# Gated attention and a token/channel mixer on one core: another order of token and channel products, and of SyncE's queue

## Chip, core and metric

The kernel runs on one core of one Trainium2 chip. The metric is the device time of one execution in microseconds, the median of several; less is better. A core has TensorE (PE in the profile, its weight loads PEld), VectorE (DVE), ScalarE (ACT), GpSimd (POOL) and SyncE (SP), each with an instruction queue of its own that it works off in order, and DMA engines that SyncE's and GpSimd's queues feed. TensorE writes its results to PSUM, from where VectorE and ScalarE take them to SBUF.

## What is computed

For each of 8 batches, an attention without softmax, gated by u, and then an MLP mixer over tokens and channels:

```python
def _attn_ref(u, v, z):                       # u, v: 8 x 3008 x 256; z: 8 x 3008 x 64
    scores = (1.0 / S) * np.matmul(z, z.transpose(0, 2, 1))
    attn = np.maximum(scores, 0.0) ** 2
    return u * np.matmul(attn, v)

def _moe_ref(x, w_tok1, w_tok2, w_ch1, w_ch2):  # token width 256, channel width 1536
    xt = x.transpose(0, 2, 1)
    h = np.maximum(xt @ w_tok1, 0.0) @ w_tok2
    u = x + h.transpose(0, 2, 1)
    return u + np.maximum(u @ w_ch1, 0.0) @ w_ch2
```

## The kernel before

**Tiles.** The 3008 rows of a batch are six query blocks of 512 (the last 448), `q` = 0 to 5 (`NQ` = 6), and as many key groups. Everything runs in bf16 with float32 sums in PSUM. PSUM is handed out in pairs of banks: a ring of three pairs, and a fourth after the first block (`ring`, `take_slot`, `bank_pair`).

**Attention.** For a query block TensorE makes the scores of a key group (`score_run`, L464), ScalarE takes them through relu (`relu`, L490 and L502), VectorE squares them (L510, L541), and TensorE multiplies by v (`av_matmul`, L691). Since scores are symmetric, only half of the blocks are computed. The others are *mirror blocks*: SyncE issues a DMA transpose of a finished block (`flip`, L561), and of the tiles under the diagonal of a diagonal block (`flip_tiles`, L553). A finished query block is gated with u (`gate`, L845): its result is kept transposed in xT, and SyncE issues a transpose of it for the token products (`turn_x`, L882). u comes by GpSimd's queue (`load_u`, L255) and is transposed on SyncE's queue too (`turn_u`, L265).

**Mixer.** For each batch: the first token product, one *piece* for each query block, all six summing into one PSUM pair (`tok1`, L1024); VectorE collects it (`collect_a`, L1040 to L1050, into a_sb); the second token product, one piece for each query block (`tok2`, L1068), which VectorE adds to xT (L1077); that sum is transposed back on SyncE's queue (`turn_u2`, L1096). Then, for each query block, six channel pieces (`ch1`, L1124, evacuated through relu into h2pre at L1162, or L1164 on VectorE) and the second channel product. The first token product and the second channel product are done with seven block products in place of eight, from sums that VectorE makes beforehand (`x_sums`, L919; `make_sums`, L1203 to L1215). The seven channel products are `product(q, k)`, L1252, in the order 1, 2, 6, 5, 7, 3, 4. They sum into two PSUM pairs: 1, 6, 7 and 4 into xb, 2, 5 and 3 into zb. After each of them VectorE adds its result to ro (`collect`, L1289), and products 6, 5, 7, 3 and 4 wait for the add on an earlier one in the same pair. The 64 odd rows at the end of a batch go by plain products (`ch2`, L1338; *residual-row pieces* below): one piece for an even batch, two for an odd one, whose second takes the rows of two batches (hs). The last query block of the last batch goes wholly by `ch2`.

**Who decides the order.** The program has no loop on the chip. A planner in Python emits all instructions in an order that it works out with costs and due times of its own. Work for VectorE, ScalarE and SyncE is put into a waiting list with `push(engine, ready, busy, latency, fn, first=...)`. `next_op` takes the item that can start first; among equals the higher `first`, then the earlier `ready`. Mixer work for TensorE stands in two lists of pieces, worked off in turn: `heads` (tok1, tok2) and `tails` (ch1, the products, ch2). `next_piece` chooses between the heads of the two lists: the list that did not go last is asked first. A piece may *open* a group that holds PSUM (the first tok1 piece, product 1) and another *closes* it (the last tok1 piece, product 4). While a group is open, its list is asked first, and no other group may open. Between the blocks of attention the planner stops for mixing at `goal`: from batch 2 on, ahead of block (b, 0), it does the pieces of query blocks 3 to 5 of batch b-2, then tok1, tok2 and query blocks 0 to 2 of batch b-1. Batch 7 is mixed at the end, and batches 0 and 1 within batch 1 and ahead of batch 2.

**So the order around the change** is, for batches 1 to 7: the products of block 4 of the batch before, with ch1 pieces of its block 5 among them; then six tok1 pieces in a run; the last ch1 piece of block 5; its ch2 pieces; then tok2 pieces of the new batch in turn with the seven products of block 5; then ch1 pieces of block 0. In `add_mixer` the tails of a block are laid down by the tuple `(0, 0, 1, 2, 0, 6, 5, 0, 7, 3, 0, 4)`, where a number is a product and 0 stands for a ch2 piece, as long as there is one, and for a ch1 piece of the next block otherwise.

Of the very last ch1 piece (batch 7, block 5) VectorE evacuates one half (L1146) and ScalarE the other (L1144). On SyncE's queue `turn_x` has `first=1`, mirror blocks have 0. `turn_u` is not put into the waiting list but emitted as soon as it is due, from the list `later`.

Of the kernel before, what the change touches and what calls it, by code (L numbers as in the profile page):

```python
# [13 lines left out]
P = 128  # L14
# [43 lines left out]
def kernel(  # L58
# [203 lines left out]
    def turn_u(b, q):  # L262
# [5 lines left out]
        on_sp(1.25)  # L268
# [566 lines left out]
    def gate(blk, dh, acc, t):  # L835
# [97 lines left out]
    opened = [None]  # L933
    before = [None]
# [58 lines left out]

    def add_mixer(b):
# [6 lines left out]
        def tok1(q, end):  # L1001
# [28 lines left out]
            if q == NQ - 1:  # L1030
                home = "fl" if b else "h2"

                def collect_a(t):
# [5 lines left out]
                    def both(to, ps, k):  # L1039
# [10 lines left out]
                    nc.vector.tensor_single_scalar(  # L1050
                        st["a"].rearrange("p m d -> p (m d)"),
                        f[:, 0:4, :].rearrange("p k d -> p (k d)"), 0.0, AX.max)
                    recent[0] = st["a"][:, 0, :1]
                    a_done.t = t
                    if b:
                        release("fl", [1], t)
                    else:
                        live["h2"] -= 1
# [53 lines left out]
        def ch1(q, c2, borrowed, end):  # L1112
            slot, _ = take_slot()
# [6 lines left out]
            hp = bank_pair(slot, "hp")  # L1120
            for r in range(2):
                cc = 2 * c2 + r
                for dc in range(DT):
                    nc.tensor.matmul(  # L1124
                        hp[:, r, :W], w_ch1_sb[:, dc, cc * P:(cc + 1) * P],
# [13 lines left out]
            if (b, q, c2) == (B - 1, NQ - 1, CHT // 2 - 1):  # L1139
                landed, freed = [], Done()  # L1140

                def evacuate_part(r, t):
                    if r:
                        nc.scalar.activation(h2[:, r, :W], hp[:, r, :W], ACT.Relu)  # L1144
# [9 lines left out]
                ring.append((freed, slot))  # L1154
# [4 lines left out]
            def evacuate(t):  # L1159
# [7 lines left out]
                if fast(q) and c2 % 2:  # L1167
                    if borrowed and q == HALF and b < B - 1:
                        late_sums.append(lambda t: make_sums(q, c2 // 2, t))
                    else:  # L1170
# [3 lines left out]
                              done=h2_done[q, c2]), slot))  # L1174
# [44 lines left out]

        def bank_of(q, k):  # L1220
# [629 lines left out]
```

## Time and profile before

| | us |
|---|---|
| median of three runs | 1124.84 (1124.3 to 1125.99) |
| the profiled execution | 1123.19 |
| its span, first to last instruction | 1121.4 |
| VectorE busy in the span | 782.4 |
| ScalarE busy in the span | 654.1 |

The profile comes from one execution. A row of the timeline has the start, the length to the end of the last instruction in it, engine, line, operation, tiles and shapes, a count, and in brackets the idle time of the engine before it with what ended it. A matmul's row reaches past the start of the next one, because matmuls are pipelined, so the length of a stretch is read from start to start. Rows of the view by stretches have the stretch, its length, the busy time and number of instructions of PE, PEld, DVE, ACT and POOL, the granted clock of TensorE, the share of the DMA engines and their GB/s. Rows of waits have who waited for whom, the total, how often and the longest. A row that ends in `x48: a/b/c, d to e` has the least, median and greatest duration in ns and the first and last start in us. SPq rows are issues of DMAs from SyncE's queue.

### The profile page before, as it was taken

What the parts mean: (1) busy time and instruction counts of PE and PEld (TensorE: products, weight loads), DVE (VectorE), ACT (ScalarE), POOL (GpSimd) and SP (SyncE); (2) the same over time, 40 slices, a digit from 0 to 9 for tenths busy, and PEclk for the clock granted to TensorE, in tenths of its full rate; (3) what the DMA queues carried; (4) which work ended last, traced back from release to release, by engine and by line L of the source; (5) the groups of instructions that cost most, each with busy time, mean ns of one, the idle gap of its engine ahead of it and who ended that gap; (6) DMA issues with size and microseconds to landing.
All of it is one profiled execution on the core that took longest, in us unless ns stands there. A gap on an engine that the chain in (4) does not pass through costs nothing.

```text
span 1121.4 us, 26909 instructions
## 1 busy us (share of the span) xinstructions
PE 1110.3 (99%) x10965; PEld 676.5 (60%) x10965; DVE 782.4 (70%) x1849; ACT 654.1 (58%) x817; POOL 164.7 (15%) x388
## 2 busy tenths in 40 slices
PE   9999999999999999999999999999999999999997
PEld 3444574766557665576555765557655576556676
DVE  6889847775757857678557775678756776557764
ACT  7998525545844467545665356753666526743363
POOL 5321100211003110031100320013200110000000
PEclk9999999999999999999999999999999999999999
DMA  9999945696986969769597896958969869684223
GB/s 177 168 185 167 203 108 124 123 167 134 191 147 130 194 119 190 141 128 205 129 173 126 149 191 141 176 117 147 209 129 159 134 145 180 131 166 96 53 77 76
DMA packets 466156, 165.52 MB, mean 148 GB/s; under 512 B 433072, under 2 KB 449008, under 8 KB 466032
## 3 DMA queue, kind: packets, MB, share of 16 engines
q1 hardware_dynamic: 436640, 131.11, 58.8%
q0 software_dynamic: 28880, 32.32, 20.8%
q8 instruction: 85, 1.39, 0.5%
q14 instruction: 39, 0.32, 0.1%
q10 hardware_dynamic: 512, 0.38, 0.1%
HBM read 65.40 MB, written 24.64 MB: 80 GB/s over the span
## 4 chain that ended last, share of the span: by engine, by line
PE 91%; DVE 4%; DMA 2%; SPq 1%; ACT 1%; issue 1%; POOL 0%; ACTq 0%; DVEq 0%; POOLq 0%
PE acc L691 39%; PE hp L1124 22%; PE xb L1252 9%; PE zb L1252 7%; PE sc L464 6%; PE a_ps L1024 3%; PE op L1338 3%; PE h_ps L1068 2%; DVE xT L1077 2%; DMA fl<-at 1%; PE first_acc L608 1%; DMA v_sb<-in_v_dram 1%; DVE res L1373 0%; ACT at L502 0%; DVE ro L1289 0%
## 5 line engine op out<-in xcount | busy, mean ns | idle before, releaser
L1162 ACT ACTIVATE h2pre<-hp 128x1024 bf16<-128x1024 f32 (+1 forms) x277 | 267.7, 1011 | 262.7 <-PE hp L1124 223.4
L691 PEld LDWEIGHTS <-v_sb 64*128 64x128 bf16 x4418 | 240.3, 94 | 217.4 <-issue 1.1
L691 PE MATMUL acc<-at,v_sb 64*128 64x512 bf16 (+1 forms) x2738 | 339.1, 374 | 0.0
L502 ACT ACTIVATE at<-sc 128x1024 bf16<-128x1024 f32 (+1 forms) x290 | 287.2, 1027 | 74.9 <-PE sc L464 56.8
L510 DVE TENSOR_TENSOR at<-at 128x1024 bf16<-128x1024 bf16 (+1 forms) x290 | 198.3, 688 | 107.4 <-ACT at L502 101.4
L1124 PE MATMUL hp<-xT,w_ch_sb 128*128 128x512 bf16 (+1 forms) x1152 | 270.6, 375 | 0.3
L691 PE MATMUL acc<-fl,v_sb 64*128 64x512 bf16 (+1 forms) x1680 | 192.1, 367 | 0.5 <-ACT at L502 0.5
L1124 PEld LDWEIGHTS <-w_ch_sb 128*128 128x128 bf16 x1152 | 105.9, 98 | 99.7 <-issue 2.6
L464 PE MATMUL sc<-zT 64*128 64x512 bf16 (+1 forms) x732 | 131.6, 359 | 1.0 <-ACT at L502 0.7
L1252 PEld LDWEIGHTS <-hsum 128*128 128x128 bf16 x1944 | 115.9, 98 | 20.1 <-issue 0.2
L1252 PEld LDWEIGHTS <-h2pre 128*128 128x128 bf16 x1458 | 88.8, 98 | 18.9
L819 ACT COPY cp<-acc 128x512 f32<-128x512 f32 (+1 forms) x94 | 54.8, 583 | 73.8 <-PE acc L691 61.4
L825 DVE TENSOR_TENSOR cp<-acc,cp 128x512 f32<-128x512 f32 (+1 forms) x94 | 63.5, 676 | 38.8 <-ACT cp L819 38.4
L1203 DVE TENSOR_TENSOR hsum<-h2pre 128x512 bf16<-128x512 bf16 (+1 forms) x132 | 53.2, 407 | 41.3 <-ACT h2pre L1162 37.1
L490 ACT ACTIVATE at<-sc 128x512 bf16<-128x512 f32 (+3 forms) x152 | 56.0, 444 | 41.5 <-PE sc L464 38.9
L1252 PE MATMUL xb<-w_mix_sb,hsum 128*128 128x128 bf16 x972 | 68.6, 219 | 0.0
L464 PEld LDWEIGHTS <-zT 64*128 64x128 bf16 x732 | 42.3, 94 | 43.7 <-issue 4.9
L541 DVE TENSOR_TENSOR at<-at 128x512 bf16<-128x512 bf16 (+3 forms) x152 | 41.5, 322 | 33.8 <-ACT at L490 33.7
L1289 DVE TENSOR_TENSOR ro<-xb,u_sb 128x256 f32<-128x256 f32 (+1 forms) x132 | 52.9, 400 | 16.9 <-PE xb L1252 15.9
L845 DVE TENSOR_TENSOR xT<-cp,uT 128x512 bf16<-128x512 f32 (+1 forms) x94 | 62.5, 665 | 0.6
L124 POOL CAST mark<-at 128x1 f32<-128x1 bf16 x24 | 9.2, 383 | 351.6 <-DVE at L510 351.6
L1077 DVE TENSOR_TENSOR xT<-xT,h_ps 128x1024 bf16<-128x1024 bf16 (+1 forms) x48 | 55.0, 1170 | 0.1
(88 smaller groups left out, 983.8 us busy)
## 6 DMA issues: line engine op xcount, KB each, us to landing
out_dram<-ro SPq DMA_DIRECT2D x37, 512.0 KB, 2.9
v_sb<-in_v_dram POOLq DMA_DIRECT2D x40, 256.0 KB, 5.1
ur<-in_u_dram POOLq DMA_DIRECT2D x40, 256.0 KB, 4.8
w_tok_sb<-in_moe_w_tok_dram POOLq DMA_DIRECT2D x10, 256.0 KB, 10.8
zs<-in_z_dram POOLq DMA_DIRECT2D x35, 64.0 KB, 4.0
at<-at SPq DMA_TRANSPOSE x114, 3.3
out_dram<-ro SPq DMA_DIRECT2D x7, 256.0 KB, 2.2
fl<-at SPq DMA_TRANSPOSE x105, 4.7
```

The costliest lines, as they stand in the source:

```text
L464: nc.tensor.matmul(sc[:, r, c0:c1], zT[h, k:k + P], zT[h, m + c0:m + c1], start=True, stop=True)
L490: nc.scalar.activation(a3[:, i, c0:c1], sc[:, r, c0:c1], ACT.Relu, scale=inv_S)
L502: nc.scalar.activation(view, sv, ACT.Relu, scale=inv_S)
L510: nc.vector.tensor_mul(view, view, view)
L691: nc.tensor.matmul(o, vs[blk.b, g][rows, i, dh * P:(dh + 1) * P], rhs, start=(dh, h) not in blk.begun, stop=stop, skip_group_check=True)
L819: nc.scalar.copy(cp[:, :W], acc[:, 1, :W])
L825: nc.vector.tensor_add(cp[:, :W], acc[:, 0, :W], cp[:, :W])
L845: nc.vector.tensor_mul(xT[:, dh, :full * P].rearrange("p (t s) -> p t s", s=P), acc[:, :full * P].rearrange("p (t s) -> p t s", s=P), uT[: ...
L1077: nc.vector.tensor_add(to, to, h[:, :, :n * P].rearrange("p h (s t) -> p h t s", t=n))
L1124: nc.tensor.matmul(hp[:, r, :W], w_ch1_sb[:, dc, cc * P:(cc + 1) * P], xT[:, dc, :W], start=(dc == 0), stop=(dc == DT - 1))
L1162: nc.scalar.activation(h2[:, :, :W], hp[:, :, :W], ACT.Relu)
L1252: nc.tensor.matmul(to[:, i * P:(i + 1) * P], lhs, weights[:, c2, :], start=(first_use and c2 == 0 and i == 0), stop=(c2 == CHT // 2 - 1), ...
```

## The change

1. A piece may *join*: the first tok1 piece of batches 1 to 7, and product 1 of the last query block. Two joining groups may be open at once, and then the lists go on in turn. So tok1 pieces and the last block's pieces alternate. `opened` becomes a list, `joined` says whether the open group is of that kind.
2. The last block's tails are laid down by `ORDER_LAST`, in which its ch2 pieces come after product 5 and after product 3, no longer ahead of product 1. The room of its h2 tiles is given back when both the products and the ch2 pieces are through (`done_with_h2`).
3. Collecting the token result becomes four items for VectorE in place of one. The PSUM pair counts as free after the third.
4. The very last ch1 piece takes two PSUM pairs, one for each half.
5. On SyncE's queue `turn_x` gets `first=-1` for blocks 0 to 3 of batches 1 to 7 (1 elsewhere, as before), and the `turn_u` that comes from `later` is put into the waiting list with `first=0`.

```diff
--- before.py
+++ after.py
@@ -47,10 +47,10 @@
     def __init__(self, cost, needs, fn, opens=False, closes=False, room=None,
-                 urgent=False, key=(0, 0), slot=None):
+                 urgent=False, key=(0, 0), slot=None, joins=False):
...
-        self.urgent, self.key = urgent, key
+        self.urgent, self.key, self.joins = urgent, key, joins
@@ -259,13 +259,14 @@
-    def turn_u(b, q):
+    def turn_u(b, q, t=None):
...
-        on_sp(1.25)
+        if t is None:
+            on_sp(1.25)
@@ -853,7 +854,8 @@
-            push("sp", t, 1.25, 7.5 if q < NQ - 1 else 12.0, lambda t: turn_x(b, q, t), first=1,
+            push("sp", t, 1.25, 7.5 if q < NQ - 1 else 12.0, lambda t: turn_x(b, q, t),
+                 first=1 if b == 0 or q >= NQ - 2 else -1,
                  room=x_room(b, q), frees=fl_free if b and q % 2 == 0 else ())
@@ -930,8 +932,8 @@
-    opened = [None]
-    before = [None]
+    opened = []
+    before, joined = [None], [False]
@@ -990,6 +992,9 @@
+    VERY_LAST = (B - 1, NQ - 1, CHT // 2 - 1)
+    ORDER_LAST = (1, 2, 6, 5, 0, 7, 3, 0, 4)
@@ -1043,21 +1048,34 @@
                     nc.vector.tensor_copy(f[:, 6, :], a_ps[:, 0, 0, :])
                     both(0, a_ps[:, 0, 1:3, :], 6)
-                    both(4, a_ps[:, 1, 1:3, :], 1)
-                    nc.vector.tensor_add(f[:, 1, :], a_ps[:, 0, 3, :], f[:, 4, :])
-                    both(2, a_ps[:, 1, 0:2, :], 5)
-                    st["a"] = sb.tile([P, 2, D], BF16, tag="a", name="a_sb", bufs=1)
...
-                ring.append((push("dve", end + 0.21, 2.2, 2.4, collect_a, first=1,
-                                  room=(home,), frees=fl_free if b else ()), st["a_slot"]))
+
+                    def both_low(t):
+                        both(4, a_ps[:, 1, 1:3, :], 1)
+                        push("dve", t - 0.05, 0.62, 0.75, both_high, first=1, done=freed)
+
+                    def both_high(t):
+                        nc.vector.tensor_add(f[:, 1, :], a_ps[:, 0, 3, :], f[:, 4, :])
+                        both(2, a_ps[:, 1, 0:2, :], 5)
+                        push("dve", t - 0.05, 0.35, 0.5, relu_a, first=1)
+
+                    def relu_a(t):
+                        st["a"] = sb.tile([P, 2, D], BF16, tag="a", name="a_sb", bufs=1)
...
+                    push("dve", t - 0.05, 0.35, 0.5, both_low, first=1)
+
+                freed = Done()
+                push("dve", end + 0.21, 0.62, 0.75, collect_a, first=1, room=(home,),
+                     frees=fl_free if b else ())
+                ring.append((freed, st["a_slot"]))
@@ -1110,19 +1128,20 @@
         def ch1(q, c2, borrowed, end):
-            slot, _ = take_slot()
+            slots = [take_slot()[0] for _ in range(1 + ((b, q, c2) == VERY_LAST))]
...
-            hp = bank_pair(slot, "hp")
+            hps = [bank_pair(slot, "hp") for slot in slots]
+            hp = hps[0]
...
-                        hp[:, r, :W], w_ch1_sb[:, dc, cc * P:(cc + 1) * P],
+                        hps[r % len(hps)][:, r, :W], w_ch1_sb[:, dc, cc * P:(cc + 1) * P],
@@ -1136,12 +1155,12 @@
-                        nc.scalar.activation(h2[:, r, :W], hp[:, r, :W], ACT.Relu)
+                        nc.scalar.activation(h2[:, r, :W], hps[1][:, r, :W], ACT.Relu)
@@ -1216,6 +1235,14 @@
+        h2_uses = [1] * NQ
+
+        def done_with_h2(q):
+
+            h2_uses[q] -= 1
+            if not h2_uses[q]:
+                live["h2"] -= CHT // 4
...
@@ -1384,7 +1411,7 @@
-                               opens=q < NQ - 1, closes=q > 0, key=(b, 0)))
+                               opens=q < NQ - 1, closes=q > 0, key=(b, 0), joins=q == 0 and b > 0))
@@ -1428,7 +1455,8 @@
-                               closes=k == 4, key=(b, 2 + q), slot=k in (1, 2)))
+                               closes=k == 4, key=(b, 2 + q), slot=k in (1, 2),
+                               joins=k == 1 and q == NQ - 1))
@@ -1443,7 +1471,8 @@
-                for k in (0, 0, 1, 2, 0, 6, 5, 0, 7, 3, 0, 4):
+                h2_uses[q] += bool(rest)
+                for k in ORDER_LAST if q == NQ - 1 else (0, 0, 1, 2, 0, 6, 5, 0, 7, 3, 0, 4):
@@ -1462,19 +1491,16 @@
-        if opened[0] is not None:
-            lists = [opened[0]] + [l for l in (heads, tails) if l is not opened[0]]
-        elif before[0] is heads:
-            lists = [tails, heads]
-        else:
-            lists = [heads, tails]
+        lists = [tails, heads] if before[0] is heads else [heads, tails]
+        if opened and not joined[0]:
+            lists.sort(key=lambda l: l is not opened[0] and not (l and l[0].joins))
...
-            if p.opens and not p.closes and opened[0] is not None:
+            if p.opens and not p.closes and opened and not (p.joins and joined[0]):
@@ -1491,7 +1517,11 @@
-        opened[0] = l if p.opens else None if p.closes else opened[0]
+        if p.opens and not any(l is o for o in opened):
+            opened.append(l)
+            joined[0] = p.joins
+        elif p.closes and not p.opens:
+            opened[:] = [o for o in opened if o is not l]
@@ -1550,8 +1580,8 @@
-        later.append((pe[0] + 11.0, lambda: gated[0] >= m - 1,
-                      lambda: turn_u(m // NQ, m % NQ)))
+        later.append((pe[0] + 11.0, lambda: gated[0] >= m - 1, lambda: push(
+            "sp", pe[0], 1.25, 5.0, lambda t: turn_u(m // NQ, m % NQ, t))))
```

More of the change, by code (lines that the diff above doesn't have):

```diff
@@ L1045, in collect_a @@
                     both(0, a_ps[:, 0, 1:3, :], 6)
[L1046 to L1060 removed]
+                    def both_low(t):
[7 more added lines that the diff above has]
+                        st["a"] = sb.tile([P, 2, D], BF16, tag="a", name="a_sb", bufs=1)
+                        nc.vector.tensor_single_scalar(
+                            st["a"].rearrange("p m d -> p (m d)"),
+                            f[:, 0:4, :].rearrange("p k d -> p (k d)"), 0.0, AX.max)
+                        recent[0] = st["a"][:, 0, :1]
+                        a_done.t = t
+                        if b:
+                            release("fl", [1], t)
+                        else:
+                            live["h2"] -= 1
+                    push("dve", t - 0.05, 0.35, 0.5, both_low, first=1)
[3 more added lines that the diff above has]
+                ring.append((freed, st["a_slot"]))
         def tok2(q, end):
@@ L1137, in keep_ends @@
                     pair["hs"][:, 2 * c2:2 * c2 + 2, r:r + TAIL], h2[:, :, W - TAIL:W])
-            if (b, q, c2) == (B - 1, NQ - 1, CHT // 2 - 1):
+            if (b, q, c2) == VERY_LAST:
                 landed, freed = [], Done()
@@ L1153, in ch1 @@
                     push(engine, at, busy, busy + 0.16, lambda t, r=r: evacuate_part(r, t))
-                ring.append((freed, slot))
+                ring.extend((freed, slot) for slot in slots)
                 release("xT", xT_uses[q])
@@ L1173, in ch1 @@
             ring.append((push(engine, end + 0.21, busy, busy + 0.16, evacuate,
-                              done=h2_done[q, c2]), slot))
+                              done=h2_done[q, c2]), slots[0]))
             if c2 == CHT // 2 - 1:
@@ L1256, in product @@
             if k == 4:
-                live["h2"] -= CHT // 4
+                done_with_h2(q)
             if k == 7:
@@ L1341, in ch2 @@
             last = i == pieces_of(q, half) - 1 and half == halves(q)[-1]
-            if last and not fast(q):
-                live["h2"] -= CHT // 4
+            if last:
+                done_with_h2(q)
             if i < pieces_of(q, half) - 1 and not apart:
@@ L1780 @@
             pick = "mixer"
-        elif hold and opened[0] is not None and tm <= t + NOW and pieces is opened[0]:
+        elif hold and opened and tm <= t + NOW and pieces is opened[0]:
             pick = "mixer"
```

1 line of the change is left out of this document (removed).

## The prediction

> **What bounds the kernel now.** I read the engine totals first, then TensorE's waits, then the stretches in which batches are mixed, and last the timeline of one such stretch.
>
> ```profile
> span 1121.4 us, 26909 instructions
> PE 1110.3 (99%) x10965; PEld 676.5 (60%) x10965; DVE 782.4 (70%) x1849; ACT 654.1 (58%) x817; POOL 164.7 (15%) x388
> PEclk9999999999999999999999999999999999999999
> PE h_ps L1068 <- DVE xT L1077: 0.9, 4, 0.5
> PE sc L464 <- ACT at L502: 0.7, 1, 0.7
> PE acc L691 <- ACT at L502: 0.5, 2, 0.3
> ```
>
> TensorE is busy in 1110.3 of 1121.4 us at the full granted clock in every slice, and the change removes no matmul. So it can win only stalls between matmuls. The rows of waits show about 2 us of them, but a busy row hides the start of a wait, because a matmul's modelled end overlaps the next one. I therefore measure from start to start: a stretch, less the starts that the same instructions take where nothing waits.
>
> Seven times, for batches 1 to 7, the second token product follows the last query block of the batch before. Each row below is that stretch: its length, then the busy time of PE, PEld, DVE, ACT and POOL.
>
> ```profile
> 228.80:236.60 7.80, 7.76 (x63) 4.46 (x61) 7.70 (x16) 0.39 (x1) 1.54 (x4) 1.00 0.90 126
> 365.10:373.60 8.50, 8.12 (x69) 4.75 (x68) 8.12 (x15) 0.00 (x0) 0.73 (x2) 1.00 0.57 107
> 502.20:510.20 8.00, 7.91 (x62) 4.47 (x60) 7.90 (x17) 0.45 (x1) 1.50 (x4) 1.00 0.73 102
> ...
> 914.40:922.90 8.50, 8.14 (x69) 4.77 (x66) 8.12 (x15) 0.00 (x0) 0.71 (x2) 1.00 0.69 123
> 1049.10:1057.10 8.00, 7.91 (x62) 4.48 (x60) 7.90 (x17) 0.43 (x1) 0.00 (x0) 1.00 0.50 94
> ```
>
> The two left out are like the rows before them. They are of two kinds: three of 8.5 us (batches 2, 4, 6), four of about 8 us. In all of them VectorE is busy for 96% or more: here VectorE is the bound, while ScalarE does next to nothing. The timeline of TensorE in the second row:
>
> ```profile
> 365.13 1.03 PE L1068 MATMUL h_ps<-w_tok_sb,a_sb 128*128 128x512 bf16 x4
> 365.99 0.50 PE L1252 MATMUL xb<-w_ch_sb,h2pre 128*128 128x128 bf16 x6
> 366.33 0.50 PE L1252 MATMUL zb<-w_ch_sb,h2pre 128*128 128x128 bf16 x6
> 366.66 1.03 PE L1068 MATMUL h_ps<-w_tok_sb,a_sb 128*128 128x512 bf16 x4
> 367.84 1.02 PE L1068 MATMUL h_ps<-w_tok_sb,a_sb 128*128 128x512 bf16 x4 [0.15 <-DVE xT L1077]
> ...
> 372.23 0.92 PE L1068 MATMUL h_ps<-w_tok_sb,a_sb 128*128 128x448 bf16 x4
> 372.98 0.50 PE L1252 MATMUL xb<-w_mix_sb,h2pre 128*128 128x128 bf16 x6
> 373.57 0.61 PE L1124 MATMUL hp<-xT,w_ch_sb 128*128 128x512 bf16 x2
> ```
>
> A token piece takes 0.86 us from start to start (365.13 to 365.99), the narrow one 0.75 (372.23 to 372.98), a channel product of the last block 0.34 (365.99 to 366.33). The stretch from 365.13 to 373.57 holds five, one and seven of these: 4.30 + 0.75 + 2.35 = 7.40 of 8.44 us. So 1.04 us are lost, 0.32 of them where the third piece waits for VectorE to free a PSUM pair (366.66 to 367.84). By the same sum a stretch of the other kind (8.0 us, with five products and one channel piece of 0.86: 4.30 + 0.75 + 1.70 + 0.86 = 7.61) loses about 0.4, and the first (7.8) about 0.2. Together 3 x 1.04 + 3 x 0.4 + 0.2 = 4.5 us: this is what the first two edits can win at most.
>
> **The change part by part.**
>
> (1) The six first token products (one list) now alternate with the last block's pieces (the other list). What that block has, by its rows:
>
> ```profile
> 356.97 0.33 PE L1024 MATMUL a_ps<-x_pair,w_tok_sb 128*128 128x128 bf16 x3
> ...
> 361.66 0.92 PE L1124 MATMUL hp<-xT,w_ch_sb 128*128 128x448 bf16 x4
> 362.42 1.56 PE L1338 MATMUL op<-w_ch_sb,h2pre 128*128 128x256 bf16 x12
> 363.82 1.47 PE L1338 MATMUL op<-w_ch_sb,hs 128*128 128x256 bf16 x12
> 362.62 0.92 ACT L1162 ACTIVATE h2pre<-hp 128x896 bf16<-128x896 f32 x1 [5.15 <-PE hp L1124]
> ```
>
> A first token piece is (361.66 - 356.97) / 6 = 0.78 us, the last channel piece 0.76, a residual-row piece 1.31 (363.82 to 365.13). The new order from T = 0 at the end of the block before: token 0.78, channel to 1.54, token to 2.32, product 1 to 2.66, token to 3.44, product 2 to 3.78, token, 6, token, 5, and the last token piece ends at 6.8. Product 1 needs the channel piece's evacuation, 1.12 us after its end (362.42 to 362.62 + 0.92): its sixth operand is there at 2.66 and is wanted at 2.60, 0.1 us lost. Every later product waits for a VectorE add of 0.28 us on the one before, and 0.78 us of token work hides it. If that cover were gone, it would cost about 0.2 us a product. In this time VectorE and ScalarE have room: between 357.5 and 361.7 the page's VectorE waits for the token products alone (the 4.27 us in the next fence).
>
> After 6.8 come a residual-row piece (to 8.11), products 7 and 3 (8.78), in batches 2, 4 and 6 a second residual piece (10.09), and product 4. They have to cover the collecting of the token result:
>
> ```profile
> 361.86 0.29 DVE L1044 COPY a_f<-a_ps 128x128 f32<-128x128 f32 x1 [4.27 <-PE a_ps L1024]
> ...
> 363.76 0.43 DVE L1050 TENSOR_SCALAR a_sb<-a_f 128x512 bf16<-128x512 f32 x1
> ```
>
> The last first-product ended at 361.66, the result stands at 364.19: 2.53 us, so 9.33 in my count. In batches 2, 4 and 6 the work up to 10.09 covers it. In the other four product 4 waits for product 7's add (from 8.45 to about 9.0, where 8.78 would be free), and the second token product starts at 9.33 to 9.5: 0.25 to 0.5 us lost.
>
> Then the six second-product pieces no longer have products among them, but they have the new batch's own channel pieces: the first may start when the first add is done, 0.86 + 0.2 + 1.13 = 2.2 us after the first piece began (1.13 is the spacing of two adds, below), or 2.8 if the residual adds stand ahead of it on VectorE. Three pieces fill 2.58. From there each pair of pieces gives TensorE 1.72 us for one add of 1.13 us, and ScalarE takes the channel evacuations.
>
> ```profile
> 366.57 1.22 DVE L1077 TENSOR_TENSOR xT<-xT,h_ps 128x1024 bf16<-128x1024 bf16 x1
> 367.70 0.28 DVE L1289 TENSOR_TENSOR ro<-xb,u_sb 128x128 f32<-128x128 f32 x1
> ```
>
> So I take 0.2 us lost where 1.04 was, and 0.45 where 0.4 or 0.2 was: 3 x 0.84 - 4 x 0.45 + 1.4 = **2.1 us won**. Bounds: 4.5 won (nothing lost any more), and the slower rival below.
>
> PSUM: the token result holds one of four pairs, the products two, so one is left from 3.44 until the collecting has read the result. The piece that needs it in that time is the residual-row piece at 6.8, and the channel piece's evacuation gave it back at 2.66.
>
> (2) Collecting in four items adds and removes no instruction; other VectorE work of 0.28 to 0.43 us may now stand between them. Cost 0 where 0.76 us of cover is left (10.09 less 9.33), one such instruction, 0.3 us, in the other four stretches. I have put that into the 0.25 to 0.5. The first batch, whose products are not joined, gets 0 with a bound of 0.3 us either way.
>
> (3) The last channel piece gets two PSUM pairs, one for each half.
>
> ```profile
> 1109.45 0.92 PE L1124 MATMUL hp<-xT,w_ch_sb 128*128 128x448 bf16 x4
> 1110.21 1.36 PE L1338 MATMUL op<-w_ch_sb,h2pre 128*128 128x256 bf16 x11
> 1110.48 0.62 DVE L1146 TENSOR_SCALAR h2pre<-hp 128x448 bf16<-128x448 f32 x1 [0.40 <-PE hp L1124]
> 1111.14 0.54 ACT L1144 ACTIVATE h2pre<-hp 128x448 bf16<-128x448 f32 x1 [1.19 <-DVE h2pre L1146]
> 1111.74 0.28 PE L1338 MATMUL op<-w_ch_sb,h2pre 128*128 128x256 bf16 x1 [0.17 <-ACT h2pre L1144]
> ```
>
> VectorE took its half only after all four matmuls and ScalarE only after VectorE. TensorE's twelfth matmul was due at 1110.21 + 12 x 0.11 - 0.11 = 1111.42 and came at 1111.74: 0.32 us lost on the path that ends the kernel. If the halves part, VectorE ends by about 1110.7 and ScalarE by 1110.95, and the 0.3 us are won; if the shared h2 tile still ties them, 0. I take **0.3**.
>
> [...]
>
> (4) SyncE's queue. Mirror blocks now go ahead of the x transposes of blocks 0 to 3 in batches 1 to 7, and of u when they were ready first.
>
> ```profile
> 592.37 2.62 SPq L882 DMA_TRANSPOSE x_pair<-xT  x2
> 595.18 1.23 SPq L265 DMA_TRANSPOSE uT<-ur  x1
> 596.52 2.89 SPq L561 DMA_TRANSPOSE fl<-at  x1
> 602.01 1.02 ACT L502 ACTIVATE at<-sc 128x1024 bf16<-128x1024 f32 x1 [1.90 <-DMA fl<-at]
> 603.09 0.39 PE L464 MATMUL sc<-zT 64*128 64x512 bf16 x2 [0.68 <-ACT at L502]
> ```
>
> Here a mirror block at 596.52 stood behind two x and one u, ScalarE waited 1.90 us for its buffer and TensorE for ScalarE. The waits quoted first give attention 0.7 + 0.5 us in three such stalls; a wait of 0.15 by its bracket was 0.32 from start to start above, so I estimate 2.0 for them. One x of 1.3 us less in front of the mirror block is most of the 1.90. I take **1.0**, with 2.0 as the one end; the other is 1 us lost, since each of seven batches gets another order of attention blocks and may meet one stall like these. Passed over are 28 x transposes and some 40 u transposes:
>
> ```profile
> L882 SPq DMA_TRANSPOSE x_pair<-xT x48: 1232/1259/2367, 24.9 to 1025.3; - x48
>   POOL ur L255: 101.6, 16
> ```
>
> The last x is issued at 1025.3, and the first token products that read it begin 4.7 us ahead of the last ch1 piece of their stretch, near 1041: 15 us of slack against some mirror blocks of 1.3 to 2.9 us. The x sums that follow run on VectorE at its lowest rank. u loads already wait on POOL's queue for the u transposes (101.6 us in 16 waits), with the v loads of the next batch behind them; a u later by one mirror block adds to a wait that costs TensorE nothing now. Both at 0.
>
> **Sum.** 2.1 + 0.3 + 1.0 = 3.4 us off the profiled execution, which took 1123.19 us with 1121.4 of span. That execution lies 1.65 us under the median of 1124.84, so I take the same difference off the median: **1121.4 us**.
>
> **The rivals.**
> *Everything fits* (0.13): no stall is left in mixing (4.5), at the end (0.3) or in attention (2.0): 6.8 us, 1118.0. For it: each stall found has other work near it. Against: four stretches lack the second residual piece.
> *The stall only moves* (0.22): the products leave the second token pieces, the VectorE-bound six adds stay, and TensorE waits as long before the first channel piece or for the collecting. Then 0 of the 2.1, with 1.3 of the rest: 1123.5. For it: VectorE busy for 96% and more. Against: with ScalarE idle there, channel pieces can fill. That the joining does not come about, because the x sums end too late, gives the same time.
> *The last free PSUM pair* (0.14), the other side: with three of four pairs held, the token result's pair comes back late behind the split collecting, and the second token pieces start with too few pairs. Price: one add and its latency, 1.13 + 0.2, in each of seven stretches: 9.3 lost for 4.5 + 0.3 won, and nothing from attention: 1129.3. It decides against the change from 4.8 / 7 = 0.7 us a stretch. Against it: the pair is idle between 2.66 and 6.8.
>
> The forecast itself has 0.51. A measurement of this kernel can tell about 0.2%, 2.25 us, from no change. Faster than 1122.6 are the forecast but for a few hundredths and the first rival: 0.62. Within are the second rival and the weak end of the forecast: 0.24. Slower 0.14. The range goes from the first rival to short of the third: 1117.8 to 1126.5; the forecast's own is 1119.4 to 1123.
>
> **What would show it.** The three stretches of batches 2, 4 and 6 from the first second-product piece on without gaps of 0.2 us, with ch1 pieces among them; ScalarE no longer at 0.00 there; L1252 rows for the last block between L1024 rows; L1146 starting before the channel piece has ended and L1144 no longer behind it; the 1.90 us wait on a mirror block gone. I am wrong if product rows of the last block show gaps, if PE waits for a PSUM pair behind L1040, or if attention shows new waits on mirror blocks, x or u.

## The result and the profile after

| | before | after |
|---|---|---|
| median, runs side by side, us | 1125.24 (1123.73 to 1129.29, 13 runs) | 1119.13 (1118.55 to 1126.02, 13 runs) |
| ratio after / before | | 0.9951, 95% interval 0.9938 to 0.9965 |
| the profiled execution, us | 1123.19 | 1119.13 |
| its span, us | 1121.4 | 1117.2 |

The change makes the kernel 0.49% faster (0.35% to 0.62%). Eleven of after's 13 runs lie between 1118.55 and 1120.29, two at 1124.36 and 1126.02. From the page of after, the totals:

```profile
PE 1108.2 (99%) x10965; PEld 682.2 (61%) x10965; DVE 782.6 (70%) x1850; ACT 655.4 (59%) x816; POOL 164.6 (15%) x388
```

The same 10965 matmuls; 4.2 us of span are gone, so the win lies between matmuls. After's waits of TensorE:

```profile
PE h_ps L1086 <- ACT at L491: 0.9, 1, 0.9
PE h_ps L1086 <- DVE xT L1095: 0.7, 1, 0.7
PE xb L1279 <- DVE ro L1316: 0.7, 4, 0.2
```

The waits on L502 (scores, now L503) and on a v load are gone, and four short ones are new, on the add of the products (L1289 before, L1316 now).

As in the prediction, stalls are measured from start to start, now over the whole span: a matmul of 512, 448, 256 or 128 columns takes 0.216, 0.189, 0.109 or 0.056 us to the next start where nothing waits (0.86 for four of 512, as before; two of attention's 64-row matmuls, which start 0.003 to 0.05 us apart, count as one), and what is over is put down to the place where it happens. In us:

| lost by TensorE | before | after |
|---|---|---|
| the seven stretches, batches 1 to 7 | 0.28, 1.11, 0.50, 1.11, 0.50, 1.11, 0.50 = 5.1 | 0.45, 0.11, 0.45, 0.11, 0.45, 0.11, 0.45 = 2.1 |
| second token product of batch 0 | 0.63 | 2.51 |
| attention, and mixing outside the stretches | 2.24 | 0.10 |
| the kernel's end | 0.33 | 0 |
| the first 12 us, and hundredths at each change of operation | 9.0 | 8.8 |
| behind the last matmul | 5.46 | 5.07 |

3.0 - 1.9 + 2.1 + 0.3 + 0.2 + 0.4 = 4.1 us: but for the rounding, the table closes on the spans. Of the 2.24 us before, 1.99 are four stalls of attention itself (0.84, 0.42, 0.31, 0.42), and after has no such stall.

The stretches of batches 2 and 3, from the first second-token piece to the end of the sixth, columns as in the prediction:

```profile
369.05:377.61 8.56, 8.56 (x47) 4.13 (x45) 7.97 (x12) 3.07 (x3) 0.72 (x2) 1.00 0.81 192
505.14:513.38 8.24, 8.24 (x42) 3.84 (x40) 7.33 (x11) 3.07 (x3) 0.00 (x0) 1.00 0.85 204
```

TensorE is busy throughout, and ScalarE, at 0.00 to 0.45 us before, works 3.07 us: three channel pieces' evacuations. The timeline of batch 2 (TensorE) and of batch 3 (TensorE, then VectorE):

```profile
367.74 1.47 PE L1365 MATMUL op<-w_ch_sb,hs 128*128 128x256 bf16 x12
369.05 1.03 PE L1086 MATMUL h_ps<-w_tok_sb,a_sb 128*128 128x512 bf16 x4
369.91 0.50 PE L1279 MATMUL xb<-w_mix_sb,h2pre 128*128 128x128 bf16 x6
370.25 1.89 PE L1086 MATMUL h_ps<-w_tok_sb,a_sb 128*128 128x512 bf16 x8
371.98 1.03 PE L1143 MATMUL hp<-xT,w_ch_sb 128*128 128x512 bf16 x4
372.84 1.03 PE L1086 MATMUL h_ps<-w_tok_sb,a_sb 128*128 128x512 bf16 x4
...
497.90 0.62 PE L1279 MATMUL xb<-w_ch_sb,h2pre 128*128 128x128 bf16 x6
498.36 0.33 PE L1029 MATMUL a_ps<-x_pair,w_tok_sb 128*128 128x128 bf16 x3
...
504.13 0.50 PE L1279 MATMUL zb<-w_ch_sb,hsum 128*128 128x128 bf16 x6
504.81 0.49 PE L1279 MATMUL xb<-w_mix_sb,h2pre 128*128 128x128 bf16 x6 [0.17 <-DVE ro L1316]
505.14 2.76 PE L1086 MATMUL h_ps<-w_tok_sb,a_sb 128*128 128x512 bf16 x12
...
504.47 0.28 DVE L1316 TENSOR_TENSOR ro<-xb,ro 128x128 f32<-128x128 f32 x1
504.67 0.42 DVE L1063 TENSOR_SCALAR a_sb<-a_f 128x512 bf16<-128x512 f32 x1
```

In batch 2 the distances are what the pieces need: 1.31, 0.86, 0.34, then pieces of 0.86 with channel pieces in turn from 371.98 on. In batch 3 two are longer: product 1 takes 0.46 (497.90 to 498.36) in place of 0.34, and product 4 starts 0.68 after product 3 (504.13 to 504.81), because the add on product 7 comes only at 504.47, behind the collecting: 0.11 + 0.34 = 0.45. These are the two losses of the prediction, where it placed them.

The end of after, engines mixed:

```profile
1105.94 0.92 PE L1143 MATMUL hp<-xT,w_ch_sb 128*128 128x448 bf16 x4
1106.59 0.62 DVE L1165 TENSOR_SCALAR h2pre<-hp 128x448 bf16<-128x448 f32 x1
1106.70 1.47 PE L1365 MATMUL op<-w_ch_sb,h2pre 128*128 128x256 bf16 x12
1106.90 0.54 ACT L1163 ACTIVATE h2pre<-hp 128x448 bf16<-128x448 f32 x1 [0.46 <-PE hp L1143]
1108.01 1.47 PE L1365 MATMUL op<-w_ch_sb,hs 128*128 128x256 bf16 x12
```

VectorE takes its half 0.65 us after the channel piece began (1.03 before), ScalarE starts 0.31 after VectorE, while VectorE is still at it, and the twelve matmuls run through in 1.31: the 0.32 are won. With a pair for each half, the two evacuations overlap by 0.31 us.

SyncE's queue at the stall of before that the prediction looked at:

```profile
591.26 1.60 SPq L562 DMA_TRANSPOSE fl<-at  x1
...
601.40 1.24 SPq L265 DMA_TRANSPOSE uT<-ur  x1
602.74 2.62 SPq L884 DMA_TRANSPOSE x_pair<-xT  x2
```

The last mirror block (fl, at 591.26) now goes out ahead of u and x; before, two x and a u stood in front of it.

### The profile page after: what moved, and what is told of

Its sections match the earlier page's. It is cut to its first block, busy times and chain, and to the rows that moved or that the text cites. A ratio compares the mean times of both kernels' runs of the same rounds, so it can differ in the third digit from the quotient of the medians.

```text
span 1117.2 us, 26931 instructions
## 1 busy us (share of the span) xinstructions
PE 1108.2 (99%) x10965; PEld 682.2 (61%) x10965; DVE 782.6 (70%) x1850; ACT 655.4 (59%) x816; POOL 164.6 (15%) x388
## 4 chain that ended last, share of the span: by engine, by line
PE 97%; DMA 1%; DVE 1%; ACT 0%; issue 0%; POOL 0%; ACTq 0%
PE acc L692 41%; PE hp L1143 22%; PE xb L1279 10%; PE zb L1279 7%; PE sc L465 6%; PE a_ps L1029 3%; PE h_ps L1086 3%; PE op L1365 3%; PE first_acc L609 1%; DMA fl<-at 1%; DMA v_sb<-in_v_dram 0%; DVE a_f L1045 0%; PE wp L205 0%; DVE xT L1095 0%; DVE a_f L1049 0%; DVE a_f L1057 0%
## 5 line engine op out<-in xcount | busy, mean ns | idle before, releaser
L692 PEld LDWEIGHTS <-v_sb 64*128 64x128 bf16 x4418 | 244.4, 94 | 213.0
L503 ACT ACTIVATE at<-sc 128x1024 bf16<-128x1024 f32 (+1 forms) x290 | 288.1, 1027 | 79.7 <-PE sc L465 72.7
L820 ACT COPY cp<-acc 128x512 f32<-128x512 f32 (+1 forms) x94 | 54.8, 583 | 62.8 <-PE acc L692 50.4
L826 DVE TENSOR_TENSOR cp<-acc,cp 128x512 f32<-128x512 f32 (+1 forms) x94 | 63.5, 676 | 35.4 <-ACT cp L820 34.6
L491 ACT ACTIVATE at<-sc 128x512 bf16<-128x512 f32 (+3 forms) x152 | 56.2, 443 | 47.2 <-PE sc L465 44.5
L1316 DVE TENSOR_TENSOR ro<-xb,u_sb 128x256 f32<-128x256 f32 (+1 forms) x132 | 52.8, 400 | 24.0 <-PE xb L1279 22.2
```

The source lines that it names most:

```text
L491: nc.scalar.activation(a3[:, i, c0:c1], sc[:, r, c0:c1], ACT.Relu, scale=inv_S)
L503: nc.scalar.activation(view, sv, ACT.Relu, scale=inv_S)
L692: nc.tensor.matmul(o, vs[blk.b, g][rows, i, dh * P:(dh + 1) * P], rhs, start=(dh, h) not in blk.begun, stop=stop, skip_group_check=True)
L820: nc.scalar.copy(cp[:, :W], acc[:, 1, :W])
L826: nc.vector.tensor_add(cp[:, :W], acc[:, 0, :W], cp[:, :W])
```

## Experiments

Four questions were open: which edit won in the stretches, which took away the attention stalls, why batch 0 lost 1.9 us, and why the median moved by 6.1 us where the spans differ by 4.2. Ratios are against runs of the kernel before on the same chip. In the profiles of `after_again`, `late_again`, `late_no_sync` and `x_before` 72 to 79 of the 10965 matmul records are missing. Each leaves a hole of one matmul's length, which is taken off before stalls are summed.

### Joining alone, and the change without the split collecting

`join_only` has the first two edits alone; `no_four` has all but the third. Their diffs against after:

```diff
# no_four: collect_a in one item, as before
-                push("dve", end + 0.21, 0.62, 0.75, collect_a, first=1, room=(home,),
...
+                ring.append((push("dve", end + 0.21, 2.2, 2.4, collect_a, first=1,
+                                  room=(home,), frees=fl_free if b else ()), st["a_slot"]))
# join_only: as no_four, and also
-                 first=1 if b == 0 or q >= NQ - 2 else -1,
+                 first=1,
-            slots = [take_slot()[0] for _ in range(1 + ((b, q, c2) == VERY_LAST))]
+            slots = [take_slot()[0] for _ in range(1)]
...
```

> The alternating lists and the last block's new order alone; collecting in one item, the last channel piece in one PSUM pair, SyncE's queue as before. Theory: the joining alone wins the mixing stalls of batches 2, 4 and 6 (1.0 us each, start to start) and nothing in the four others, so 3.0 us against the kernel before (ratio 0.997), and the second token product of batch 0 keeps its 0.6 us of stalls. Rival: the gain needs the split collecting; then the three stretches keep 0.5 us or more each and the gain is under 1.5 us.

> The whole change without the split collecting. Theory: batch 0's second token product has 0.6 us of stalls again and nothing else is lost: 1.9 us faster than the changed kernel, ratio to the kernel before 0.9935 to 0.994. Rival: the joined stretches need the split; then they lose 0.3 us or more each and the sum is no better than the changed kernel.

`join_only`: 1119.84 us (1119.43 to 1123.71), 0.9957 (0.9939 to 0.9976). `no_four`: 1118.84 (1117.98 to 1119.91), 0.9944 (0.9923 to 0.9965). In both the stretches of batches 2, 4 and 6 lose 0.11 us, the four others 0.72, batch 0 loses 0.63 as before, and attention has none of the stalls of before (of the 0.6 us that `no_four` loses elsewhere, 0.39 are one wait of a channel product in the mixing; what `join_only` loses near 105 us is told in the last section). The three long stretches are thus won by the joining alone, 1.0 us each. The four short ones become worse by it, and get 0.27 of the 0.72 back by the split. The waits of TensorE in `no_four`, and its timeline of VectorE in batch 3, show how:

```profile
PE h_ps L1074 <- DVE a_sb L1056: 1.8, 4, 0.4
...
502.94 0.43 DVE L1056 TENSOR_SCALAR a_sb<-a_f 128x512 bf16<-128x512 f32 x1
503.28 0.28 DVE L1304 TENSOR_TENSOR ro<-xb,ro 128x128 f32<-128x128 f32 x1
```

In one item the collecting holds VectorE until 503.28, the add on product 7 comes behind it and with it product 4, so that nothing is left to cover the token result. In four items the add gets in ahead of the last (504.47 before 504.67), and product 4 covers part. So in these profiles edit 3 wins 4 x 0.27 = 1.1 us in the stretches and loses 1.9 in batch 0. `no_four` was to be 1.9 us faster than the change; the medians, taken on different chips, are 0.3 us apart and the intervals overlap, so its rival came nearer.

### The split collecting alone

`four_only` is before with the third edit only.

```diff
-                    both(4, a_ps[:, 1, 1:3, :], 1)
...
+                    push("dve", t - 0.05, 0.35, 0.5, both_low, first=1)
```

> Only the collecting of the token result in four items. Theory: it lets a square of attention in between the items in batch 0, scores run one pair ahead, and batch 0's second token product loses 2.5 us in place of 0.6; nothing is won elsewhere: 1.9 us slower, ratio 1.002. Rival: batch 0 stays at 0.6, because SyncE's queue is the cause; then no change.

1122.71 us (1121.83 to 1126.92), 0.9977 (0.9962 to 0.9993): the expectation was wrong in sign. Batch 0 lost only 1.03, the short stretches won 0.06 to 0.14 each, and the attention stalls of before are gone here too, with SyncE's queue untouched by any rule. (Its profile is that of an execution of 1126.92 us, which lost 5 us near 100 us; the last section has it.) The size of batch 0's loss therefore does not follow from the split by itself, but from the schedule that comes out of it.

### Batch 0

The timelines of after, and of a kernel that collects in one item in batch 0 alone (`late_again`, below), VectorE, ScalarE and TensorE:

```profile
117.14 0.68 DVE L511 TENSOR_TENSOR at<-at 128x1024 bf16<-128x1024 bf16 x1
...
115.68 10.52 ACT L503 ACTIVATE at<-sc 128x1024 bf16<-128x1024 f32 x10 [4.16 <-PE sc L465]
126.56 1.04 ACT L503 ACTIVATE at<-sc 128x1024 bf16<-128x1024 f32 x1
129.82 0.98 ACT L491 ACTIVATE at<-sc 128x512 bf16<-128x512 f32 x2 [2.22 <-DMA fl<-at]
130.69 0.59 ACT L820 COPY cp<-acc 128x512 f32<-128x512 f32 x1
130.85 1.02 PE L1086 MATMUL h_ps<-w_tok_sb,a_sb 128*128 128x512 bf16 x4 [0.86 <-ACT at L491]
131.92 1.21 DVE L1095 TENSOR_TENSOR xT<-xT,h_ps 128x1024 bf16<-128x1024 bf16 x1
```

```profile
118.96 7.28 ACT L503 ACTIVATE at<-sc 128x1024 bf16<-128x1024 f32 x7 [0.87 <-PE sc L465]
126.60 1.96 ACT L503 ACTIVATE at<-sc 128x1024 bf16<-128x1024 f32 x2
128.42 0.62 ACT L820 COPY cp<-acc 128x512 f32<-128x512 f32 x1
128.13 3.63 PE L1092 MATMUL h_ps<-w_tok_sb,a_sb 128*128 128x512 bf16 x15
130.09 1.21 DVE L1101 TENSOR_TENSOR xT<-xT,h_ps 128x1024 bf16<-128x1024 bf16 x1
```

In the first fence a square gets between two items of the collecting (117.14). ScalarE runs ten relus without a pause, and when the second token product begins (128.09) it has reached the relu of a narrow diagonal block (L491), whose buffer a mirror block's DMA still reads: 2.22 us. The copy L820 of the finished accumulator stands behind it in ScalarE's queue, and TensorE waits 0.86 for the PSUM pair that the relu reads. In the second fence ScalarE pauses 0.87 us after two relus and is one relu behind, and the copy starts at 128.42. The copy's delay goes on to VectorE, which adds it to the accumulator (L826) before it adds the first result of the second token product: that add starts at 131.92 in the first fence, at 130.09 in the second. Of the 2.51 us lost in after, 1.03 are the wait for ScalarE, and the other 1.48 are waits for VectorE behind it.

```diff
# four_late, late_again: against after
-                    push("dve", t - 0.05, 0.35, 0.5, both_low, first=1)
+                    if b:
+                        push("dve", t - 0.05, 0.35, 0.5, both_low, first=1)
+                        return
...
+                whole = push("dve", end + 0.21, 0.62 if b else 2.2, 0.75 if b else 2.4,
...
+                ring.append((freed if b else whole, st["a_slot"]))
```

> The whole change, with the collecting in one item in batch 0 and in four in batches 1 to 7. Theory: batch 0's second token product is back at 0.6 us and the joined stretches keep 0.45 and 0.11: 1.9 us less than the changed kernel up to TensorE's last matmul, ratio to the kernel before 0.993. Rival: the shifted plan meets other waits in attention for as much, and nothing is won.

> The changed kernel itself once more, as the yardstick for the two kernels run with it. Theory (the first batch's loss and the kept stalls are fixed by the order that is written out): the same rows again, 2.5 us lost with the second token product of batch 0, 0.45 or 0.1 in the joined stretches, attention below 0.3, ratio to the kernel before 0.995. Rival (the first batch's loss is an accident of when one mirror block lands): batch 0 loses a different amount, by over 0.5 us, with the same order of instructions.

> The changed kernel with the token result collected in one item in batch 0, in four in the joined batches; run again beside the changed kernel. Theory (collecting in four items costs in the first batch alone): about 1.3 us (2.5 less 1.2 in batch 0) faster than the changed kernel on the same chip, ratio to before 0.993 to 0.994. Rival (what the first batch wins is given back in attention, where its profile lost 0.95 us instead of 0.1): within 0.5 us of the changed kernel, ratio 0.995.

`four_late`: 1117.94 us (1117.75 to 1118.61, 5 runs), 0.9927 (0.9914 to 0.9939). Then, on one chip, `after_again`: 1119.26 (1118.95 to 1123.23, 6 runs), 0.9951 (0.9935 to 0.9968), and `late_again`: 1117.85 (1117.59 to 1118.41, 6 runs), 0.9934 (0.9919 to 0.9949). The two sets of six runs do not overlap, the medians are 1.4 us apart: one item in batch 0 and four elsewhere beats the change. Batch 0 lost 1.48 us in `after_again`, 1.23 and 0.63 in the two runs of the other kernel, against 2.51 in after. For batch 0 the rival of `after_again` came true, then: the order is fixed, the amount goes with when the mirror block lands. In `after_again` the five mirror blocks were issued from 119.79 in place of 120.65, ScalarE waited a microsecond less, TensorE no longer waited for it, and the 1.48 us on VectorE stayed:

```profile
128.71 0.98 ACT L491 ACTIVATE at<-sc 128x512 bf16<-128x512 f32 x2 [1.20 <-DMA fl<-at]
```

Of the 1.4 us between the medians, these two profiles put 0.85 into batch 0. That of `after_again` also has two waits of a channel product in the mixing, 0.42 and 0.56 us, where `late_again` has one of 0.15; whether batch 0 brings them too is not shown.

### The short stretches

The second residual piece that batches 1, 3, 5 and 7 lack can't be had, but the one they have can come later, ahead of product 4.

```diff
# four_late_even: against four_late
-                for k in ORDER_LAST if q == NQ - 1 else (0, 0, 1, 2, 0, 6, 5, 0, 7, 3, 0, 4):
+                for k in (ORDER_LAST if b % 2 else (1, 2, 6, 5, 7, 3, 0, 4)) if q == NQ - 1 else (0, 0, 1, 2, 0, 6, 5, 0, 7, 3, 0, 4):
```

> As the run before, and in stretches with one residual-row piece that piece comes between products 3 and 4 in place of after product 5, so that it covers the wait of product 4 on product 7's add. Theory: 0.34 us of stall at that place go in batches 1, 3, 5 and 7, and the wait for the collected token result comes up in its place for about 0.2: 0.5 us less in all. Rival: the whole 0.34 moves to the second token product's first piece, no change.

1119.6 us (1118.59 to 1124.03), 0.9946 (0.9931 to 0.996). The four stretches lost 0.85 each where `four_late` lost 0.45, so neither theory nor rival came true. By the waits of this kernel the loss is now on the token result itself, in place of an add:

```profile
PE h_ps L1092 <- DVE a_sb L1063: 2.3, 4, 0.6
```

### SyncE's queue

`sync_only` is before with the fifth edit alone, `x_before` has its half on x alone, `no_sync` is after without it, `late_no_sync` is `four_late` without it.

```diff
# sync_only: against before; x_before has the first of the two
-            push("sp", t, 1.25, 7.5 if q < NQ - 1 else 12.0, lambda t: turn_x(b, q, t), first=1,
+            push("sp", t, 1.25, 7.5 if q < NQ - 1 else 12.0, lambda t: turn_x(b, q, t),
+                 first=1 if b == 0 or q >= NQ - 2 else -1,
...
+        later.append((pe[0] + 11.0, lambda: gated[0] >= m - 1, lambda: push(
+            "sp", pe[0], 1.25, 5.0, lambda t: turn_u(m // NQ, m % NQ, t))))
# no_sync, late_no_sync: both taken back
```

> Only SyncE's queue is changed (x and u let mirror blocks pass). Theory: the four waits in attention behind mirror blocks go (2.0 us start to start), mixing stays at its 5.1 us, batch 0's second token product stays at 0.6: 2 us faster, ratio 0.998. Rival: the new queue order is what makes the 1.9 us of new stalls in batch 0's second token product; then these show up here, and the gain is about 0.

> The kernel before, with one edit: mirror blocks ahead of the x transposes of query blocks 0 to 3 in batches 1 to 7 (u as before, nothing joined, collecting in one item). Theory (the attention stalls of the kernel before come from the last mirror block standing behind two x in SyncE's queue): the mirror block goes ahead of x, attention loses 0.9 us or less instead of 2.24, mixing 5.1 as before; 1.3 us faster, ratio 0.999 to 0.997. Rival (it takes the u transpose as well, or the queue's order is only a shift of the plan): the 1.9 us wait of ScalarE on a mirror block stays, attention 2 us, ratio 1.000.

> The whole change without the SyncE part: x and u are placed as before. Theory: attention is without the four waits anyway (0.1 to 0.6 us left there), mixing as in the changed kernel (2.1 us), batch 0's second token product loses about 1.0 as with the split collecting alone: no slower than the changed kernel, ratio to the kernel before 0.994 to 0.996. Rival: the SyncE part wins 1 to 2 us in attention; then this is 1 to 2 us slower than the changed kernel, with mirror-block waits behind x and u.

> The same (one item in batch 0, four in the joined batches) without the edit on SyncE's queue: x ahead of mirror blocks everywhere, as before. Theory (with the joined products the mirror blocks stand ahead of x in any case, so the queue's edit is worth nothing on top): no difference from the kernel with it by more than 1 us, attention below 1 us, ratio 0.993. Rival (the edit is worth 1.0 us by itself, as in the prediction): 1 us or more slower than the kernel with it, with mirror waits of 0.5 us and more back, ratio 0.994 to 0.995.

| | median, us | ratio | attention, and mixing outside the stretches, lost, us | of it in attention's stalls |
|---|---|---|---|---|
| sync_only | 1122.24 (1121.3 to 1126.41) | 0.9974 (0.9956 to 0.9991) | 0.93 | none |
| x_before | 1123.64 (1122.58 to 1128.4) | 0.9987 (0.9972 to 1.0001) | 0.95 | 0.56 |
| no_sync | 1120.17 (1118.72 to 1122.98) | 0.9949 (0.9934 to 0.9964) | 0.26 | none |
| late_no_sync | 1118.19 (1117.22 to 1118.77) | 0.9936 (0.9922 to 0.9949) | 1.10 | none |

By itself the edit wins 1.3 us outside the stretches (2.24 less 0.93). All four stalls of attention are gone, 1.99 us, with the one that the prediction looked at; 0.68 us come back as one wait of a channel product for VectorE's add, in the mixing near 354 us:

```profile
PE xb L1267 <- DVE ro L1304: 0.5, 1, 0.5
```

Whether the edit brings that wait is open, since `join_only` and `four_only`, which lack the edit, have waits of this kind too, of 0.35 and 0.33 us at other places. With the half on x alone the stall shrinks: in `x_before` the mirror block goes out ahead of u and both x, 3.1 us earlier than before; ScalarE waits for it all the same, but TensorE loses 0.56 us there instead of 1.26 (the timeline of SyncE and ScalarE):

```profile
593.41 1.58 SPq L562 DMA_TRANSPOSE fl<-at  x1
595.47 1.24 SPq L265 DMA_TRANSPOSE uT<-ur  x1
...
597.80 3.77 ACT L503 ACTIVATE at<-sc 128x1024 bf16<-128x1024 f32 x4 [2.10 <-DMA fl<-at]
```

So theory and rival each have a part, and the interval of `x_before` reaches 1: its gain in time stays open. On top of the joining the edit is worth nothing that these runs can tell: `no_sync` has the ratio that was expected (only its batch 0 lost 1.68 us in place of about 1.0), `late_no_sync` against `late_again` is 0.3 us on one chip, and none of the 1.10 us that it lost is a wait on a mirror block. SyncE's timeline of `join_only`, which has no rule for this queue, says why:

```profile
592.53 1.58 SPq L562 DMA_TRANSPOSE fl<-at  x1
...
597.14 1.32 SPq L884 DMA_TRANSPOSE x_pair<-xT  x1
```

The mirror block stands ahead of x without being told: with the mixing planned otherwise, other items fall due first.

### The kernel before once more

> The kernel before once more, for a second profile. In the first four runs every variant lost the four waits of attention (2.0 us), also those that leave SyncE's queue alone, and the kernel before ran up to 5 us over its profiled execution. Theory: those waits hang on how a mirror block's DMA falls in time, so a second profile has them at other places or of another size, and mixing is the same to 0.1 us. Rival: they are fixed by the order of SyncE's queue; then the same four waits stand at the same places (0.84, 0.42, 0.31, 0.42).

1125.1 us (1121.77 to 1130.81, 10 runs), 0.9999 (0.9983 to 1.0015). This profile is of an execution of 1130.81 us, 7.6 above that of the first profile; 6.2 of them lie in the span. The seven stretches lost the same to a hundredth, batch 0 lost 1.05 us in place of 0.63, and attention with the rest of the mixing 8.0 in place of 2.2. Two of the four stalls of the first profile stand at the same place here, 1.2 and 0.4 us long (at 608.59 and 610.80; 602.02 and 603.87 in the first), two are gone, and seven are new, the longest of 2.5 us at 106. Theory and rival each have a part, the theory the larger. The waits of TensorE and of ScalarE in it:

```profile
PE sc L464 <- ACT at L502: 3.6, 3, 2.3
ACT at L502 <- DMA fl<-at: 11.9, 6, 3.5
```

In the first profile the second of these rows had 8.7 us in five waits. What differs between these two executions of one kernel is, for the most part, when mirror blocks land. All runs of before here lie between 1121.6 and 1131.0 us, those of `four_late` and `late_again` between 1117.6 and 1118.6.

## Why the prediction was right, and where it was not

**Mixing** was right in its mechanism and a little small: 2.1 us forecast, 3.0 measured. The two kinds of stretch keep 0.11 and 0.45 where it said 0.2 and 0.45, and over the somewhat longer stretch used now they had lost 5.1, not 4.5. Product 1 waits 0.11 (forecast 0.1), and product 4 waits for product 7's add, as said. `join_only` shows the three long stretches to be the joining's.

**Collecting in four items.** That products' adds may stand between the items was right, and in the stretches this wins 1.1 us. "The first batch, whose products are not joined, gets 0 with a bound of 0.3 us either way" failed: it lost 1.9 us in the profile, 0.9 in another, and a kernel without it there is 1.4 us faster. The step looked at VectorE's queue alone. What got between the items was a square of the attention, and the loss arose two queues on, at ScalarE, behind a buffer that a DMA held: 1.03 us directly, the rest through the copy that came late to VectorE.

**The last channel piece**: 0.3 forecast, 0.33 measured, in every kernel that has the edit and in none that has not.

**SyncE's queue**: "I take 1.0", with 2.0 as the one end. Attention won that end, 1.99. The stall was the right one, but the gain is not the edit's alone: any of the three larger edits took it away by another order (`join_only`, `four_only`, `sync_only`), and with the joining in, this one adds nothing measurable. TensorE had none of the new waits on x or u.

**The sum** was 3.4 us from profile to profile; measured, 1123.19 - 1119.13 = 4.06. The larger part of the miss of 2.3 us lies in "I take the same difference off the median". The profiled execution of before lay 1.65 us under the median, most likely because the stalls on mirror blocks vary and were small in it: the second profile, slower by 7.6 us, lost 5.8 more in attention and the rest of the mixing. The change takes these stalls away, and the offset is gone too: after's profiled execution is its median. 0.66 + 1.65 = 2.3. That no profile of a median execution of before was taken leaves this a reading, not a proof. The 1119.13 us lie just under the 1119.4 that the prediction gave as the forecast's own end. And that the sum of the profiles came within 0.7 us is in part luck: mixing and attention gave 0.9 and 1.0 us more than forecast, and batch 0 took 1.9 back.

**The rivals.** "Everything fits" came true in attention and at the end, not in the four short stretches. "The stall only moves" fell in the stretches; in batch 0, which it did not name, a stall did arise. "The last free PSUM pair": no product or token piece of the stretches waited for a pair held by the collecting.

## What to carry to other kernels

Where a planner fixes the order, splitting one item lets whatever is ready in between, from every stage; look one queue further for what then comes early, and split only where the cover is wanted. A stall on a DMA that comes and goes between runs belongs to the median, not to one profile: take a second profile before the difference between the two is carried through a forecast. When an edit and its neighbours remove the same stall, test each alone and each left out; only the latter says what it is worth in the whole.

## What was not expected of the hardware

Two gaps of TensorE went with half the granted clock for 3.41 us, a third of about the same length did not. In `join_only` TensorE stood 2.11 us waiting for ScalarE, in `four_only` 2.31 us waiting for a mirror block, in the second profile of before 2.29 us. Below are TensorE's row behind the gap in `join_only` and in before, and stretches around the gaps of all three. In a stretch's row the number behind the comma is the time that TensorE was busy, and the one ahead of the last two the granted clock:

```profile
107.62 0.61 PE L465 MATMUL sc<-zT 64*128 64x512 bf16 x2 [2.11 <-ACT at L503]
104.13:107.54 3.41, 1.38 (x14) 0.57 (x11) 0.96 (x3) 1.00 (x2) 1.01 (x1) 1.00 1.21 166
107.54:110.95 3.41, 3.33 (x16) 1.35 (x17) 2.28 (x4) 2.41 (x4) 0.53 (x1) 0.50 1.17 262
```

```profile
100.47:103.89 3.42, 1.11 (x12) 0.56 (x11) 3.42 (x8) 1.02 (x1) 1.45 (x1) 1.00 1.21 179
103.89:107.30 3.41, 3.41 (x18) 1.50 (x16) 0.37 (x2) 1.02 (x1) 0.14 (x1) 0.50 1.28 135
```

```profile
108.87 0.39 PE L464 MATMUL sc<-zT 64*128 64x512 bf16 x2 [2.29 <-ACT at L502]
107.00:110.00 3.00, 1.13 (x12) 0.65 (x13) 1.12 (x3) 2.20 (x3) 0.00 (x0) 1.00 1.03 230
110.00:113.00 3.00, 3.00 (x32) 1.64 (x29) 1.85 (x3) 2.02 (x3) 0.53 (x1) 1.00 1.61 261
```

In `join_only` and `four_only` the clock is half for 3.41 us: eight matmuls of 512 columns take 1.70 us there (108.00 to 109.70 in `join_only`) and 0.86 in before (109.09 to 109.95). In before it stays whole, 1.00 from 107 to 113 us. It fell at 107.54 in `join_only`, 0.08 us ahead of the end of the gap, and at 103.89 in `four_only`, 1.05 us behind it (102.84). The length of the gap alone does not tell the three apart, since the one of 2.29 us lies between the two others. What decided is not shown.
